# Chunked attention and a feed-forward on one core: the opening stretch in another order, with more zero products

## The chip, the cores and the metric

The kernel runs on one core of one Trainium2 chip. The metric is the device time of one execution in microseconds. Before the change it is 223.09 us, the median of three runs (223.05 to 223.10).

## The reference

Four sequences (B) of 768 tokens with 8 heads of 64. Each chunk of 32 queries sees 8 memory keys and the keys from 16 before to 8 after the chunk; the result, put together over the heads, goes through a normalization and two weight matrices, and is added to itself.

```python
for c in range(nc):                       # chunks of 32
    l_start, r_end = max(0, c_start - 16), min(S, c_end + 8)
    k_full = concat(mem_k, k[l_start:r_end]); v_full = concat(mem_v, v[l_start:r_end])
    a = softmax(q_c @ k_full.T / 8)
    out[c] = a @ v_full
x = out, heads side by side               # (4, 768, 512)
xn = (x - mean) / sqrt(var + 1e-6) * g_ln
y = x + relu(xn @ w_ch1) @ w_ch2          # 512 -> 2048 -> 512
```

## The kernel before, in words

**Tiles and units.** The tokens are 24 tiles of 128 (6 for each sequence). The feed-forward goes by units u = 0 to 7 of three tiles. W1 (`w1c`) and W2 (`w2c`) lie in SBUF as four quarters each. For a unit, "up" makes the 2048 hidden columns (xT times a quarter of W1, then a relu into `rT`), "down" multiplies them by W2 and adds up over the quarters. Attention of later tiles is put between these steps.

**Attention of a tile.** `scores` are 16 products of 64 x 104 x 64 into a PSUM pair `att`; `soften` are two exponentials on ScalarE (into `AT`); `values` are 16 products with V, followed on VectorE by a reciprocal, a scaling that also sums, and the negative mean; `norm` subtracts the mean and multiplies by `gb` (the gain, spread over 128 partitions by two products `spread_g`); `turn_x` transposes the result into `xT`, for the first tiles by four products on TensorE and a copy on VectorE. The division by the standard deviation comes at the very end, since relu lets it through.

**Keys and queries.** They arrive in blocks of 256 tokens. A block of raw data (`st`) is rearranged by one copy (`mix`, or `mix_raw` in pieces for the first block, into `iv`), transposed by eight products (`transpose_block`, `first_q`), and copied out of PSUM: keys by `window` and `key_left`, `key_right` into `KT` with its overlapping windows; queries by `part_q` or `whole_q` into `QR`. The memory keys go through `mem_keys` (16 small transposes), `memT` and `mem_cols` into KT's last columns; the memory values through `v_mem` into V.

**The order.** There is no scheduler: each engine carries out its instructions in the order in which the program calls the helpers, and semaphores carry the data dependencies. The program has a front written out by hand (lines 557 to 627) and a plan of 28 steps for each unit (`at`, `attend`). Unit 0 is special: `up_tile(u, c, i, eng)` makes all 512 hidden columns of quarter c for one tile i alone, in 16 products of 128 columns, so that work can begin when the first tile is done. The front calls it for tiles 0 and 1 of all four quarters, and the loop for tile 2 in steps 12 to 15. From step 16 come the down products. PSUM for up and down products are four banks `mm`, taken in turn by `slot`.

**Zero products.** `warm(n, m, p)` multiplies zeros by zeros into a bank that nobody reads. They are there to keep TensorE active while it has nothing else to do.

**Loads.** `first_load`, the memory keys, the gain and the memory values go by the queues of SyncE, ScalarE and GpSimd at the very start; everything else goes by GpSimd's queue in one fixed order: second key block, V, W1's first quarter, V, W1's second, second query block, W1's third, V, W1's last, third key block, V, W2's first quarter, and so on. Each issue there waits for the landing of the eighth load before it.

Of the kernel before, what the change touches and what calls it, by code (L numbers as in the profile page):

```python
# [15 lines left out]
def kernel(  # L16
# [12 lines left out]
    nc = tc.nc  # L29
# [60 lines left out]
    def dram(t, offset, pattern):  # L90
        return bass.AP(tensor=t.tensor, offset=offset, ap=[list(p) for p in pattern])

    def free(ap, off, pattern, parts=None):
        p = list(ap.ap[0]) if parts is None else [ap.ap[0][0], parts]
        return bass.AP(tensor=ap.tensor, offset=ap.offset + off, ap=[p] + [list(x) for x in pattern])
# [4 lines left out]
    def copy(eng, out, in_):  # L100
        if eng is nc.scalar:
            eng.copy(out=out, in_=in_)
        else:
            eng.tensor_copy(out=out, in_=in_)
# [28 lines left out]
    def v_mem(b, g0, g1, eng):  # L133
        src = memv16[96:W, b, :, :]
        copy(eng, free(V[b % 2][96:W, g0:g1, :, :], 0, [[H * VW, g1 - g0], [1, H * VW]]),
             bass.AP(tensor=src.tensor, offset=src.offset,
                     ap=[list(src.ap[0]), [0, g1 - g0], [1, H * VW]]))
# [12 lines left out]
    def mem_keys():  # L150
        p = slot("att")
        pv = as16(p[:, 0, :])
        for m in range(8):
            for par in range(2):
                nc.tensor.matmul(
                    out=pv[64 * par : 64 * par + 64, 32 * m : 32 * m + 32],
                    lhsT=memk16[:, 64 * m : 64 * m + 64], rhs=identity[0:32, 0:32],
                    is_transpose=True, start=True, stop=True, tile_position=(0, 64 * par),
                )
        mem_slot.append(pv)  # L160
# [52 lines left out]
    def transpose_block(b, blk, which, banks):  # L213
        i = pick(iv, ("b", b, blk, which))
        for r in range(8):
            pv = banks[r // 4 if len(banks) == 2 else 0]
            c = 128 * (r % 4 if len(banks) == 2 else r)
            nc.tensor.matmul(  # L218
                out=pv[:, c : c + 128], lhsT=i[:, 128 * r : 128 * r + 128], rhs=identity,
                is_transpose=True, start=True, stop=True,  # L220
            )
# [26 lines left out]
    def part_q(b, blk, half, pv, eng):  # L248
        copy(eng, free(QR[b % 2], 1024 * blk + 64 * half, [[128, 8], [1, 64]]),
             free(pv, 64 * half, [[128, 8], [1, 64]]))  # L250

    def mix_raw(which, srcs, half, eng, lo=0, hi=128):

        o = pick(iv, ("b", 0, 0, which))[lo:hi, :]
        r0, n = (0, 8) if half is None else (4 * half, 4)
        for par in range(2):
            copy(eng, free(o, 128 * r0 + 64 * par, [[128, n], [1, 64]]),
                 free(srcs[par][lo:hi, :], 64 * r0, [[64, n], [1, 64]]))

    def first_q(half):  # L260

        i = pick(iv, ("b", 0, 0, 1))
        rows = slice(64 * half, 64 * half + 64)
        for r in range(8):
            c = 128 * r + 64 * half
            nc.tensor.matmul(
                out=Q0[0][:, c : c + 64],
                lhsT=i[rows, 128 * r : 128 * r + 128], rhs=identity[rows, rows],
                is_transpose=True, start=True, stop=True, tile_position=(64 * half, 0),
            )  # L270
# [33 lines left out]
    def soften(b, t, c):  # L304
        p = score_slot[b, t]
        nc.scalar.activation(  # L306
            out=free(AT[t % 3], 32 * c, [[64, 16], [1, 32]]),
            in_=free(p, 4 * c, [[64, 16], [1, 4], [8, 8]], W),
            func=ACTF.Exp, bias=band[0:W, c : c + 1], scale=0.125,
        )  # L310
# [45 lines left out]
    def turn_x(b, t):  # L356
        i = NT * b + t
        dst = xT[(i // 3) % 2][:, :, 128 * (i % 3) : 128 * (i % 3) + 128]
        if i not in ON_PE:
            nc.sync.dma_start_transpose(out=dst, in_=xn[i % 4])  # L360
            return
        p = slot("att")
        pv = as16(p[:, 0, :])
        for dt in range(4):
            nc.tensor.matmul(  # L365
                out=pv[:, 128 * dt : 128 * dt + 128],
                lhsT=xn[i % 4][:, 128 * dt : 128 * dt + 128], rhs=identity,
                is_transpose=True, start=True, stop=True,
            )
        nc.vector.tensor_copy(out=dst, in_=free(pv, 0, [[128, 4], [1, 128]]))  # L370
# [10 lines left out]
    def relu(eng, o, p):  # L381
        if eng is nc.scalar:
            nc.scalar.activation(out=o, in_=p, func=ACTF.Relu)  # L383
        else:
            nc.vector.tensor_scalar(out=o, in0=p, scalar1=0.0, scalar2=None, op0=ALU.max)  # L385
# [12 lines left out]
    def up_tile(u, c, i, eng):  # L398
        p = slot("mm")
        for k_ in range(4):  # L400
            for dt in range(4):
                nc.tensor.matmul(  # L402
                    out=p[:, 128 * k_ : 128 * k_ + 128],
                    lhsT=free(w1c[c][:, dt, :], k_, [[4, 128]]),
                    rhs=xT[u % 2][:, dt, 128 * i : 128 * i + 128],
                    start=(k_ == 0 and dt == 0), stop=(k_ == 3 and dt == 3),
                )
        relu(eng, rT[c][:, :, 128 * i : 128 * i + 128], free(p, 0, [[128, 4], [1, 128]]))

    down_slot = {}  # L410

# [40 lines left out]
    def warm(n, m=512, p=None):  # L452
        p = mm[3] if p is None else p
        for _ in range(n):
            nc.tensor.matmul(out=p[:, 0:m], lhsT=zero[:, 0:128], rhs=zero[:, 0:m], start=True, stop=True)
# [4 lines left out]
    def first_load(which, par, lo, hi, eng):  # L460
        eng.dma_start(
            out=raws[which][par][4 * lo : 4 * hi, :],
            in_=dram((k, q)[which], 4 * par * HS + 512 * lo, [[512, hi - lo], [HS, 4], [1, 512]]),
        )

    first_load(0, 0, 0, 32, nc.sync)
    first_load(0, 1, 0, 32, nc.scalar)
    first_load(1, 0, 0, 16, nc.sync)
    first_load(1, 1, 0, 16, nc.gpsimd)
    nc.sync.dma_start(out=memkf, in_=dram(mem_k, 0, [[512, 32], [1, 512]]))  # L470
    nc.sync.dma_start(out=grow, in_=dram(moe_g_ln, 0, [[512, 1], [1, 512]]))

    nc.sync.dma_start(out=xs[5][96:W, :], in_=dram(mem_v, 0, [[64, 8], [512, 8], [1, 64]]))
# [80 lines left out]
        cols = slice(256 * half, 256 * half + 256)  # L554
        nc.tensor.matmul(out=mm[3][:, cols], lhsT=gone, rhs=grow[:, cols], start=True, stop=True)

    warm(7)
    mix_raw(0, raws[0], 0, dve)
    mix_raw(0, raws[0], 1, act)
    transpose_block(0, 0, 0, K0)  # L560
    mix_raw(1, raws[1], 0, dve, 0, 64)
    mix_raw(1, raws[1], 1, act, 0, 64)
    copy(dve, memk16, memkf)
    first_q(0)
    mem_keys()
    window(0, 0, K0, 0, dve)
    window(0, 0, K0, 1, act)
    part_q(0, 0, 0, Q0[0], act)
# [9 lines left out]
    mix(0, 1, 0, dve)  # L578
    spread_g(1)
    first_q(1)  # L580
    part_q(0, 0, 1, Q0[0], dve)
    copy(act, gb, mm[3])
    values(0, 0)
    norm(0, 0)
    window(0, 0, K0, 2, act)
# [2 lines left out]
    window(0, 1, Q0, 0, act)  # L588
    window(0, 1, Q0, 1, act)
    key_right(0, 3, act)  # L590
    turn_x(0, 0)
    warm(1, 512, mm[1])
    scores(0, 1)
    soften(0, 1, 0)
    soften(0, 1, 1)
    v_mem(0, 2, 4, dve)
    turn["mm"] = 3
    up_tile(0, 0, 0, act)
    values(0, 1)
    norm(0, 1)  # L600
    window(0, 1, Q0, 2, dve)
    window(0, 1, Q0, 3, act)
    key_left(0, 4, dve)
    warm(1, 512, mm[1])
    mix(0, 1, 1, dve)
    up_tile(0, 1, 0, act)
    turn_x(0, 1)
    Q1 = [as16(slot("mm")) for _ in range(2)]
    transpose_block(0, 1, 1, Q1)
    whole_q(0, 1, Q1)  # L610
    up_tile(0, 0, 1, act)
    scores(0, 2)
    soften(0, 2, 0)
    soften(0, 2, 1)
    v_mem(0, 4, 6, dve)
    up_tile(0, 1, 1, dve)
    up_tile(0, 2, 0, dve)
    values(0, 2)
    norm(0, 2)
    up_tile(0, 2, 1, act)  # L620
    mix(0, 2, 0, dve)
    up_tile(0, 3, 0, act)
    turn_x(0, 2)
    up_tile(0, 3, 1, dve)
    total(cnt[:, 1:2], 0, 80)
    total(cnt[:, 2:3], 96, W)
    nc.vector.tensor_tensor(out=cnt[:, 1:2], in0=cnt[:, 1:2], in1=cnt[:, 2:3], op=ALU.add)
    plan = {}

    def at(u, step, fn, *args):  # L630
# [97 lines left out]
    for u in range(8):  # L728
        for step in range(U):
            if step < 16:  # L730
                if u == 0:
                    if step >= 12:
                        up_tile(0, step - 12, 2, dve if step % 2 else act)
                else:
                    up(u, step)
            elif u == 0:
                c, i = divmod(step - 16, 3)
                down(u, i, c)
            else:
                i, c = divmod(step - 16, 4)  # L740
                if u == 7 and i == 2:
                    if c == 0:
                        last_down(u, i)
                else:
                    down(u, i, c)
            for fn, args in sorted(plan.get((u, step), ()), key=lambda x: x[0] is not soften or x[1][2] == 0):
                fn(*args)
# [30 lines left out]
```

## Time and profile before

| | |
|---|---|
| time | 223.09 us |
| span of the profile | 221.3 us |
| TensorE busy | 212.3 us (96%), 1969 products |
| VectorE, ScalarE, GpSimd busy | 133.2, 102.1, 97.5 us |
| largest groups on TensorE | L417 down 83.0 us, L391 up (units 1 to 7) 78.5, L402 up tiles of unit 0 13.4 |
| chain that ended last | TensorE 80% of the span |

TensorE is the engine to look at. Its row in the 40 slices is 9 (90% or more) almost everywhere except in the first four slices. Column "PEclk" of that table shows what a throttle granted, not the rate at which the products really ran: that has to be read from the distance of like products. In the timelines, a line gives the start, the length, the engine, the line of the program, what is written and read, the shape and the number of instructions, and in brackets the idle time of the engine just before and what ended it. In the windows, each engine has its busy time and the number of its instructions, and the last three columns are the granted clock, the share of the DMA engines that was busy, and GB/s.

### The profile page before, as it was taken

What the parts mean: (1) busy time and instruction counts of PE and PEld (TensorE: products, weight loads), DVE (VectorE), ACT (ScalarE), POOL (GpSimd) and SP (SyncE); (2) the same over time, 40 slices, a digit from 0 to 9 for tenths busy, and PEclk for the clock granted to TensorE, in tenths of its full rate; (3) what the DMA queues carried; (4) which work ended last, traced back from release to release, by engine and by line L of the source; (5) the groups of instructions that cost most, each with busy time, mean ns of one, the idle gap of its engine ahead of it and who ended that gap; (6) DMA issues with size and microseconds to landing.
All of it is one profiled execution on the core that took longest, in us unless ns stands there. A gap on an engine that the chain in (4) does not pass through costs nothing.

```text
span 221.3 us, 4995 instructions
## 1 busy us (share of the span) xinstructions
PE 212.3 (96%) x1969; PEld 131.4 (59%) x1969; DVE 133.2 (60%) x329; ACT 102.1 (46%) x217; POOL 97.5 (44%) x171
## 2 busy tenths in 40 slices
PE   5978999999999999999999999999999999999993
PEld 1656986557755576546754576446754666456553
DVE  5755686587879768735756687716754377234221
ACT  3554558516783167623771176424841466103200
POOL 7954496798897991303832893200011011100000
PEclk9999999999999999999999999999999999999999
DMA  6999999999979999277995899693112211210012
GB/s 169 173 190 195 197 195 192 183 140 222 157 100 151 222 184 156 45 175 168 145 153 102 102 156 187 64 204 99 27 24 79 90 23 27 71 69 29 0 47 95
DMA packets 72274, 27.70 MB, mean 125 GB/s; under 512 B 60346, under 2 KB 68282, under 8 KB 72251
## 3 DMA queue, kind: packets, MB, share of 16 engines
q0 software_dynamic: 46080, 14.71, 62.9%
q1 hardware_dynamic: 26026, 12.41, 25.5%
q8 instruction: 15, 0.25, 0.5%
q10 hardware_dynamic: 144, 0.26, 0.4%
q14 instruction: 9, 0.07, 0.1%
HBM read 30.28 MB, written 6.29 MB: 165 GB/s over the span
## 4 chain that ended last, share of the span: by engine, by line
PE 80%; DVE 0%; issue 0%; DVEq 0%
PE mm L417 34%; PE mm L391 34%; PE att L296 5%; PE att L317 3%; PE mm L439 2%; PE att L218 1%; PE mm L218 1%; PE att L365 0%; DVE osb L444 0%; DVEq L444 0%
## 5 line engine op out<-in xcount | busy, mean ns | idle before, releaser
L417 PE MATMUL mm<-w2c,rT 128*128 128x512 f16 x368 | 83.0, 379 | 0.0
L391 PE MATMUL mm<-xT,w1c 128*128 128x384 f16 x448 | 78.5, 327 | 0.0
L391 PEld LDWEIGHTS <-w1c 128*128 128x128 f16 x448 | 49.0, 114 | 22.0
L417 PEld LDWEIGHTS <-rT 128*128 128x128 f16 x368 | 34.9, 98 | 39.4
L385 DVE TENSOR_SCALAR rT<-mm 128x384 f16<-128x384 f32 (+1 forms) x61 | 34.3, 567 | 25.7 <-PE mm L391 22.3
L383 ACT ACTIVATE rT<-mm 128x384 f16<-128x384 f32 (+1 forms) x63 | 31.4, 503 | 38.6 <-PE mm L391 22.6
L306 ACT ACTIVATE AT<-att,band 104x512 f16<-104x512 f32 x48 | 31.3, 684 | 29.8 <-PE att L296 29.8
L128 POOL DMA_DIRECT2D V<-in_v_dram x48 | 38.8, 822 | 7.2 <-DMA w1c<-in_moe_w_ch_dram 4.3
L426 DVE SCALAR_TENSOR_TENSOR osb<-mm,rstd,xs 128x512 f32<-128x512 f32 x23 | 17.2, 749 | 33.5 <-PE mm L417 27.5
L348 POOL TENSOR_SCALAR veps<-sq 128x1 f32<-128x1 f32 x24 | 7.4, 310 | 63.4 <-ACT junk L342 49.8
L342 ACT ACTIVATE junk<-xs,nmean 128x512 f16<-128x512 f32 x24 | 17.3, 722 | 15.4 <-DVE nmean L331 13.4
L337 DVE SCALAR_TENSOR_TENSOR xn<-xs,nmean,gb 128x512 f16<-128x512 f32 x24 | 17.9, 747 | 0.5
L325 DVE SCALAR_TENSOR_TENSOR xs<-att,rec 128x512 f32<-128x512 f32 x24 | 16.6, 691 | 0.8
L296 PE MATMUL att<-QR,KT 64*104 64x64 f16 x384 | 16.0, 235 | 0.1
L296 PEld LDWEIGHTS <-KT 64*104 64x104 f16 x384 | 12.7, 135 | 4.7 <-issue 3.4
L352 POOL TENSOR_TENSOR rstd<-veps,mhalf 128x1 f32<-128x1 f32 x24 | 14.5, 603 | 2.0
L120 POOL DMA_DIRECT2D st<-in_q_dram x22 | 13.1, 618 | 4.1 <-DMA st<-in_q_dram 2.3
L120 POOL DMA_DIRECT2D st<-in_k_dram x22 | 12.8, 605 | 2.8 <-DMA w1c<-in_moe_w_ch_dram 2.7
L402 PE MATMUL mm<-xT,w1c 128*128 128x128 f16 x192 | 13.4, 232 | 0.0
L324 DVE RECIPROCAL rec<-att 128x8 f32<-128x8 f32 x24 | 4.9, 206 | 13.2 <-PE att L317 12.8
L317 PEld LDWEIGHTS <-AT 104*64 104x64 f16 x384 | 8.4, 114 | 7.3 <-issue 3.9
L402 PEld LDWEIGHTS <-w1c 128*128 128x128 f16 x192 | 12.3, 118 | 0.5 <-issue 0.3
(77 smaller groups left out, 144.0 us busy)
## 6 DMA issues: line engine op xcount, KB each, us to landing
out_dram<-osb SPq DMA_DIRECT2D x23, 256.0 KB, 2.2
V<-in_v_dram POOLq DMA_DIRECT2D x40, 96.0 KB, 5.7
st<-in_k_dram POOLq DMA_DIRECT2D x22, 128.0 KB, 5.9
st<-in_q_dram POOLq DMA_DIRECT2D x22, 128.0 KB, 6.6
w1c<-in_moe_w_ch_dram POOLq DMA_DIRECT2D x4, 512.0 KB, 11.1
w2c<-in_moe_w_ch_dram POOLq DMA_DIRECT2D x4, 512.0 KB, 8.5
V<-in_v_dram POOLq DMA_DIRECT2D x8, 80.0 KB, 5.4
xT<-xn SPq DMA_TRANSPOSE x17, 2.4
```

Source lines behind the costliest of these rows:

```text
L120: nc.gpsimd.dma_start(out=s[:, 512 * par : 512 * par + 512], in_=dram((k, q)[which], (b * H + 4 * par) * HS + blk * 256 * D, [[512, 32], [ ...
L128: nc.gpsimd.dma_start(out=V[b % 2][lo:hi, g, :, 0:64], in_=dram(v, b * H * HS + (64 * g - 16 + lo) * D, [[64, hi - lo], [HS, H], [1, 64]]),)
L296: nc.tensor.matmul(out=p[0:W, par, (4 * gg + j) * 64 : (4 * gg + j) * 64 + 64], lhsT=KT[b % 2][rows, 2 * t + gg, j, :], rhs=free(QR[b % 2] ...
L306: nc.scalar.activation(out=free(AT[t % 3], 32 * c, [[64, 16], [1, 32]]), in_=free(p, 4 * c, [[64, 16], [1, 4], [8, 8]], W), func=ACTF.Exp, ...
L337: nc.vector.scalar_tensor_tensor(out=xn[i % 4], in0=xs[i % 9], scalar=nmean[t], in1=gb, op0=ALU.add, op1=ALU.mult,)
L342: nc.scalar.activation(out=junk, in_=xs[(NT * b + t) % 9], func=ACTF.Square, bias=nmean[t], scale=1.0, accum_out=sq[t],)
L383: nc.scalar.activation(out=o, in_=p, func=ACTF.Relu)
L385: nc.vector.tensor_scalar(out=o, in0=p, scalar1=0.0, scalar2=None, op0=ALU.max)
L391: nc.tensor.matmul(out=p, lhsT=free(w1c[c][:, dt, :], i, [[4, 128]]), rhs=xT[u % 2][:, dt, 128 * lo : 128 * (lo + n)], start=(dt == 0), st ...
L402: nc.tensor.matmul(out=p[:, 128 * k_ : 128 * k_ + 128], lhsT=free(w1c[c][:, dt, :], k_, [[4, 128]]), rhs=xT[u % 2][:, dt, 128 * i : 128 * ...
L417: nc.tensor.matmul(out=p, lhsT=rT[c][:, k_, 128 * i : 128 * i + 128], rhs=w2c[c][:, k_, :], start=(c == 0 and k_ == 0), stop=(c == 3 and k ...
L426: nc.vector.scalar_tensor_tensor(out=o, in0=p, scalar=rstd[t % 9], in1=xs[t % 9], op0=ALU.mult, op1=ALU.add,)
```

## The change

It reorders the front and moves some operations to other engines; what is computed and the loads stay, apart from one place in SyncE's queue. The parts:

1. Ten zero products instead of seven before the first transposes, and one more ahead of the memory keys' transposes.
2. The memory keys are loaded second on SyncE's queue, cast before the first queries, and transposed before them.
3. The copy of the gain `gb` from PSUM goes from ScalarE to VectorE, before the copy of the second half of the first queries.
4. `scores(0, 1)` and its exponentials come before `turn_x(0, 0)`, with three zero products ahead of them instead of one behind the turn; the last key windows of block 1 come before the first up tile, and the zero product after `values(0, 1)` goes.
5. `mix` of the second query block goes from VectorE to ScalarE.
6. The relu of `up_tile(0, 1, 0)` goes from ScalarE, where it stood right after its products, to VectorE after `scores(0, 2)`; for this `up_tile` can give back its operands instead of issuing the relu.
7. `up_tile(0, 0, 1)` goes from before `scores(0, 2)` to after it.
8. The two up tiles of W1's last quarter for tiles 0 and 1 leave the front. The loop takes six up tiles from step 10 on: tile 2 for the first three quarters, then all three tiles for the last.

Parts 1 and 2 are meant to have TensorE at its full rate early and the first scores sooner; 3 to 7 to fit the order to that; 8 so as not to wait for the load of W1's last quarter.

```diff
-        relu(eng, rT[c][:, :, 128 * i : 128 * i + 128], free(p, 0, [[128, 4], [1, 128]]))
+        pair = rT[c][:, :, 128 * i : 128 * i + 128], free(p, 0, [[128, 4], [1, 128]])
+        if eng is None:
+            return pair
+        relu(eng, *pair)
...
+    nc.sync.dma_start(out=memkf, in_=dram(mem_k, 0, [[512, 32], [1, 512]]))
     first_load(1, 0, 0, 16, nc.sync)
     first_load(1, 1, 0, 16, nc.gpsimd)
-    nc.sync.dma_start(out=memkf, in_=dram(mem_k, 0, [[512, 32], [1, 512]]))
...
-    warm(7)
+    warm(10)
     mix_raw(0, raws[0], 0, dve)
     mix_raw(0, raws[0], 1, act)
     transpose_block(0, 0, 0, K0)
+    copy(dve, memk16, memkf)
+    warm(1)
+    mem_keys()
     mix_raw(1, raws[1], 0, dve, 0, 64)
     mix_raw(1, raws[1], 1, act, 0, 64)
-    copy(dve, memk16, memkf)
     first_q(0)
-    mem_keys()
...
     first_q(1)
+    copy(dve, gb, mm[3])
     part_q(0, 0, 1, Q0[0], dve)
-    copy(act, gb, mm[3])
     values(0, 0)
...
     key_right(0, 3, act)
-    turn_x(0, 0)
-    warm(1, 512, mm[1])
+    warm(3, 512, mm[1])
     scores(0, 1)
     soften(0, 1, 0)
     soften(0, 1, 1)
+    turn_x(0, 0)
     v_mem(0, 2, 4, dve)
-    turn["mm"] = 3
-    up_tile(0, 0, 0, act)
-    values(0, 1)
-    norm(0, 1)
     window(0, 1, Q0, 2, dve)
     window(0, 1, Q0, 3, act)
     key_left(0, 4, dve)
-    warm(1, 512, mm[1])
-    mix(0, 1, 1, dve)
-    up_tile(0, 1, 0, act)
+    turn["mm"] = 3
+    up_tile(0, 0, 0, act)
+    mix(0, 1, 1, act)
+    values(0, 1)
+    norm(0, 1)
+    late = up_tile(0, 1, 0, None)
     turn_x(0, 1)
     Q1 = [as16(slot("mm")) for _ in range(2)]
     transpose_block(0, 1, 1, Q1)
     whole_q(0, 1, Q1)
-    up_tile(0, 0, 1, act)
     scores(0, 2)
     soften(0, 2, 0)
     soften(0, 2, 1)
+    relu(dve, *late)
     v_mem(0, 4, 6, dve)
+    up_tile(0, 0, 1, act)
     up_tile(0, 1, 1, dve)
-    up_tile(0, 2, 0, dve)
     values(0, 2)
     norm(0, 2)
+    up_tile(0, 2, 0, act)
     up_tile(0, 2, 1, act)
+    turn_x(0, 2)
     mix(0, 2, 0, dve)
-    up_tile(0, 3, 0, act)
-    turn_x(0, 2)
-    up_tile(0, 3, 1, dve)
...
+    TILES = ((0, 2), (1, 2), (2, 2), (3, 0), (3, 1), (3, 2))
...
                 if u == 0:
-                    if step >= 12:
-                        up_tile(0, step - 12, 2, dve if step % 2 else act)
+                    if step >= 10:
+                        up_tile(0, *TILES[step - 10], dve if step % 2 else act)
```

## The prediction

> **What bounds the kernel now.** I read the busy table in 40 slices first (TensorE 9 in every slice from the fifth on), then the waits of TensorE, then windows cut where its work changes, then its timeline, then the DMA issues.
>
> The waits of TensorE (time, times, longest) and the windows (busy time of each engine in each stretch):
>
> ```profile
> PE mm L218 <- DVE iv L104: 2.0, 2, 1.2
> PE att L365 <- DVE xn L337: 1.7, 3, 1.2
> ```
> ```profile
> 22.19:29.04 6.85, 6.52 (x125) 6.07 (x126) 4.58 (x11) 3.83 (x7) 4.07 (x7) 1.00 1.42 198
> 29.04:34.65 5.61, 5.61 (x107) 5.45 (x105) 4.32 (x15) 3.56 (x12) 5.40 (x13) 1.00 1.58 190
> 34.65:49.20 14.55, 14.32 (x152) 7.80 (x151) 9.96 (x27) 7.58 (x16) 11.12 (x20) 1.00 1.33 171
> ```
>
> From 22 us on TensorE hardly stops; after 44 us no wait of it is listed at all. So the end moves by what the front (up to the first down product at 34.65) gains or loses, and by nothing else. The front's own timeline on TensorE (start, length, line, operation):
>
> ```profile
> 15.65 0.91 PE L296 MATMUL att<-QR,KT 64*104 64x64 f16 x16
> 16.49 1.90 PE L402 MATMUL mm<-xT,w1c 128*128 128x128 f16 x16
> ...
> 22.19 0.62 PE L218 MATMUL mm<-identity,iv 128*128 128x128 f16 x8 [0.79 <-DVE iv L104]
> 22.65 1.06 PE L402 MATMUL mm<-xT,w1c 128*128 128x128 f16 x16
> 23.64 0.65 PE L296 MATMUL att<-QR,KT 64*104 64x64 f16 x16
> 24.22 1.98 PE L402 MATMUL mm<-xT,w1c 128*128 128x128 f16 x32
> 26.12 0.44 PE L317 MATMUL att<-V,AT 104*64 104x65 f16 x16
> 26.50 1.98 PE L402 MATMUL mm<-xT,w1c 128*128 128x128 f16 x32
> 28.80 0.40 PE L365 MATMUL att<-identity,xn 128*128 128x128 f16 x4 [0.33 <-DVE xn L337]
> 29.04 1.95 PE L402 MATMUL mm<-xT,w1c 128*128 128x128 f16 x32
> ```
>
> Two things are to be seen. The same 16 products of an up tile take 1.90 at 16.49 and 1.06 at 22.65: TensorE runs at half speed until some point near 20 us (the granted-clock column says 1.00 throughout and doesn't show it). And between 22.65 and 34.65 every chain of other engines is covered by up tiles, of 0.89 us each (1.95 for two, less the drain).
>
> The loads are on GpSimd's queue. Issued at 8.89 and 9.43, the second query block (st) lands 10.5 us later; W1's last quarter is issued at 14.87:
>
> ```profile
> st<-in_q_dram POOLq DMA_DIRECT2D x2, 128.0 KB, 10.5
> ```
> ```profile
> w1c<-in_moe_w_ch_dram POOLq DMA_DIRECT2D x1, 512.0 KB, 11.5
> ```
>
> So the query block is complete at 19.95 and W1's last quarter at 26.4. The order of loads is not changed, and each issue waits for an earlier load, not for TensorE, so I keep both.
>
> [...] (1.90-0.31)/15 = 106 ns a product before, (1.06-0.22)/15 = 56 ns after. [...] the trace has TensorE busy from 10.0 to 13.5 with transposes and narrow products, and still at half speed afterwards[...]. [...] VectorE's rearrangement of the query block starts at 21.45, 1.5 us after the block landed, behind a norm and two copies. [...] ScalarE's relus here take 0.60 for 512 columns and 0.49 for 384, or 0.86.
>
> **The change part by part.**
>
> *Zero products, mem keys first.* Ten products at 427 ns from 1.18 end at 5.45; the first transposes start at 5.55, when VectorE has the keys, so three more cost nothing. One more stands in the wait for the mem keys' cast. The aim is the clock: [...] Both branches are carried. With mem keys cast ahead of the queries, VectorE reaches the first scores about 0.35 sooner (9.0 instead of 9.39).
>
> *gb on VectorE.* A 128x512 f32 read from PSUM is 0.69 there (row of L385), between the cast of the second queries and values(0,0), where ScalarE had 0.58. It eats what the earlier scores gave VectorE: values' reciprocal at 12.35 cold or 11.85 hot, against 12.63. ScalarE's key copies, freed of gb, still wait for the second block's transposes and end at about 14.5 cold, 13.5 hot.
>
> *Scores ahead of turn_x, three zero products.* scores(0,1) then starts at 14.55 cold or 13.6 hot, against 15.65. But cold, turn_x after it makes up(0,0) start at 16.5, as before; hot, 15.0. W1's second quarter (issued at 8.14, 10.7 later, so 18.9) then stops a hot TensorE in any case, for up(1,0).
>
> *Query rearrangement on ScalarE.* It no longer stands behind the norm: it starts when the block lands, 19.98. ScalarE has not run a 1024-column copy here; bounds are VectorE's 0.69 and two 512-column copies, 1.2. I take 0.60 + 512 x 0.86 ns = 1.04: done at 21.04, transposes at 21.1 hot. Cold, turn_x(0,1) (about 21.03, as before) is in front and they start at 21.26. Before: 22.19. So this step gains 0.9 to 1.1, and the clock decides only 0.16 of it. The landing is what caps it.
>
> *What follows the transposes.* Here is the loss. Before, up(0,1) lay between the transposes and scores(0,2), and two tiles of W1's last quarter, (3,0) and (3,1), lay before tile 2's first product. Now the first is behind the scores and the others are behind three tiles of tile 2. With intervals of the old timeline, hot:
> - Transposes to query copy done on ScalarE: 22.19 to 23.43, so 21.1 to 22.33; scores(0,2) at 22.38. TensorE has 0.45 of work in it and then waits 0.83.
> - Scores to both exponentials done: 0.69 + 1.26, at 24.33. TensorE goes on after 0.58, does up(0,1) and up(1,1) in 1.90, and starts values(0,2) at 24.86. ScalarE relus up(0,1) behind the exponentials, nobody waits for it.
> - VectorE has relu(1,1), 0.75 from 24.97, queued ahead of the reciprocal: that starts at 25.66; reciprocal to norm takes 1.90 (26.84 to 28.74): 27.56. The deferred relu of up(1,0) runs at 22.0 and meets up(1,1)'s need of its buffer at 23.9 without a wait.
> - TensorE: 0.38 for values, two tiles 1.79, at 27.03; turn_x at 27.62. A wait of 0.59, in which W1's last quarter has been there since 26.4 and isn't asked for.
> - turn_x 0.23, then VectorE's copy: 0.50 to its start, 0.42, 0.06: tile 2 may start at 28.60. A wait of 0.75.
> - From there, six tiles instead of five: 29.04 to 34.65 was 5.61 with five tiles, the eight transposes and the scores; with one more, 6.50. First down product at 35.10.
>
> Against 34.65 this is +0.45 hot and +0.6 cold. The 1.1 gained at 21.1 is paid back with 1.7 of waits that were covered before. After 34.65 the order on all engines is the same, TensorE is busy 14.32 of 14.55, and the second matrix' first quarter (landing at 31.4) is not reached sooner, so the shift is carried to the end. I take +0.5: 223.09 + 0.5 = 223.6.
>
> **The rivals.**
> - *A wash.* If values(0,2) isn't held by up(1,1) and the reciprocal not by the relu, the chain runs on its own links: values at 24.4, norm done at 26.75, tile 2 free at about 28.0 after the two tiles; six tiles then end at 34.5. With the cold variant's 0.16 this is between -0.15 and 0: 223.0. For it: each hold is under half a microsecond and rests on a place in a queue. Against: the order on both engines is fixed and the durations are of this trace.
> - *Faster.* The gain of the transposes stands and TensorE isn't starved, because the query block lands sooner than 19.95 or the chain is much shorter: 223.09 - 1.1 = 222.0. For it: the waits of 0.79 and 1.16 us go[...]. Against: what runs at half speed there hangs on casts, copies and landings; every load in flight shares queues that are busy in every slice.
> - *The clock goes wrong.* A hot TensorE with little to do from 16.4 to 21.1 falls back[...] Against: before had waits of 0.4 and 0.8 within 2 us and stayed at full speed.
>
> **How the numbers follow.** Starved as worked out 0.50, a wash 0.22, faster 0.13, clock 0.15. The predicted time is the first case's, 223.6. Its unknowns are the ScalarE copy (0.69 to 1.2: -0.35 to +0.15), the branch of the clock (0.16) and the landing (some 0.3 either way). Slower by over 0.45 us (0.2%): most of the first case (0.40 of 0.50) and all of the clock, 0.55; within: the rest of the first and most of the wash, 0.27; faster: 0.13 and the wash's edge, 0.18. The range runs from the better half of the faster side of the wash to the clock's edge, 222.4 to 224.4, leaving out most of the faster case and half of the clock's.
>
> **What would show it.** Right: the second block's query transposes at 21.0 to 21.3, ended by ScalarE's copy that started within 0.1 of the landing near 19.95; three new waits of TensorE between 21.5 and 28.6, of about 0.8 (ScalarE's or VectorE's query copy), 0.6 (norm) and 0.75 (copy of xT); first down product near 35.1; the stretch from it to the end as long as before. Wrong: a down product before 34.5, or transposes of the queries before 20.8 (the landing is not the cap), or up tiles of 1.9 us after 20.3 (the clock). Whether an up tile at 15 to 16.5 takes 1.06 or 1.90 tells if the zero products did what they are for; by these sums it matters for 0.16 us.

## The result and the profile after

The changed kernel takes 224.29 us (median of 4 runs, 223.93 to 224.94) against 223.07 us (223.04 to 223.10): ratio 1.0058, 95% interval 1.0035 to 1.0081. Run again beside the next experiments it is 224.28 against 223.19, ratio 1.0040 (1.0024 to 1.0055). It is slower, by 1.1 to 1.2 us.

Waits of TensorE in the trace of after (us in total, times, longest):

```profile
PE mm L402 <- DVE xT L370: 1.5, 2, 1.0
PE mm L458 <- DVE zero L511: 1.2, 1, 1.2
PE att L296 <- ACT QR L102: 1.1, 2, 0.7
PE att L365 <- DVE xn L337: 1.1, 1, 1.1
```

The timeline of TensorE in the trace of after, from the second scores to tile 2:

```profile
15.89 1.05 PE L402 MATMUL mm<-xT,w1c 128*128 128x128 f16 x16 [0.51 <-DVE xT L370]
16.88 0.44 PE L317 MATMUL att<-V,AT 104*64 104x65 f16 x16
17.25 1.09 PE L402 MATMUL mm<-xT,w1c 128*128 128x128 f16 x16
19.43 0.40 PE L365 MATMUL att<-identity,xn 128*128 128x128 f16 x4 [1.09 <-DVE xn L337]
19.66 0.61 PE L218 MATMUL mm<-identity,iv 128*128 128x128 f16 x8
20.95 0.65 PE L296 MATMUL att<-QR,KT 64*104 64x64 f16 x16 [0.67 <-ACT QR L102]
21.53 3.28 PE L402 MATMUL mm<-xT,w1c 128*128 128x128 f16 x32
24.74 0.65 PE L317 MATMUL att<-V,AT 104*64 104x65 f16 x16
25.32 1.98 PE L402 MATMUL mm<-xT,w1c 128*128 128x128 f16 x32
27.43 0.40 PE L365 MATMUL att<-identity,xn 128*128 128x128 f16 x4
28.83 2.87 PE L402 MATMUL mm<-xT,w1c 128*128 128x128 f16 x48 [1.00 <-DVE xT L370]
```

Up tiles run at full rate from 15.9 on (1.05), so the opening is faster: the second query block's transposes start at 19.66 instead of 22.19. Behind them TensorE waits 0.67 and 1.00 us, and the two tiles at 21.53 take 3.28 us instead of 1.98: half rate again. Windows of that trace, cut at the clock's edges (us, TensorE busy and products, granted clock, DMA share, GB/s):

```profile
11.70:15.12 3.41, 3.41 (x36) 0.50 1.68 193
15.12:18.53 3.41, 2.70 (x52) 1.00 1.22 200
18.53:21.94 3.41, 1.84 (x35) 1.00 1.68 186
21.94:25.36 3.41, 3.41 (x45) 0.50 1.46 193
```

Since the first loads land up to 0.7 us apart from one trace to the next, the traces are best compared by distances. F is the start of the first transposes, S that of the second query block's transposes, D that of the first down product (from the timelines, in us; D to the end is the span less D; each ratio is to before as run beside it):

| trace | F to S | S to D | D to end | time, ratio to before (95%) |
|---|---|---|---|---|
| before | 16.64 | 12.46 | 186.65 | |
| before, second trace | 16.27 | 12.45 | 186.65 | |
| after | 13.74 | 15.71 | 186.8 | 224.29, 1.0058 (1.0035 to 1.0081) |
| after, second trace | 15.31 | 14.38 | 186.7 | 224.28, 1.0040 (1.0024 to 1.0055) |
| last quarter back | 14.99 | 13.14 | 186.9 | 222.88, 0.9989 (0.9975 to 1.0004) |
| kept busy | 15.84 | 14.38 | 186.7 | 224.50, 1.0055 (1.0036 to 1.0075) |
| seven zeros | 14.13 | 15.87 | 186.7 | 224.43, 1.0055 (1.0038 to 1.0073) |
| old tail | 15.71 | 12.67 | 186.6 | 222.48, 0.9968 (0.9955 to 0.9980) |
| old tail, gb on ScalarE | 13.84 | 12.68 | 186.8 | 221.51, 0.9930 (0.9903 to 0.9957) |
| the same, filled | 14.25 | 12.87 | 186.9 | 221.69, 0.9924 (0.9910 to 0.9938) |
| before, ten zeros | 16.16 | 12.45 | 186.9 | 222.69, 0.9982 (0.9971 to 0.9992) |
| before, query block on ScalarE | 16.39 | 12.45 | 186.7 | 223.03, 0.9993 (0.9980 to 1.0006) |
| before, windows and query block | 15.52 | 12.74 | 186.6 | 222.64, 0.9966 (0.9953 to 0.9978) |

D to the end hardly moves: everything is decided before the first down product, and the change gains in the first column and loses more in the second. A gain in the first column is not all the change's own: the second traces of after and of before differ from the first ones too.

### The profile page after: what moved, and what is told of

It reads as the page before. It is cut to its first block, busy times and chain, and to the rows that moved or that the text cites. A ratio compares the mean times of both kernels' runs of the same rounds, so it can differ in the third digit from the quotient of the medians.

```text
span 222.2 us, 5004 instructions
## 1 busy us (share of the span) xinstructions
PE 212.9 (96%) x1974; PEld 131.7 (59%) x1974; DVE 133.8 (60%) x329; ACT 102.8 (46%) x217; POOL 98.5 (44%) x171
## 4 chain that ended last, share of the span: by engine, by line
PE 79%; DVE 0%; issue 0%; DVEq 0%
PE mm L420 34%; PE mm L391 34%; PE att L296 5%; PE att L317 3%; PE mm L442 2%; PE att L218 1%; PE mm L218 1%; PE att L365 0%; DVE osb L447 0%; DVEq L447 0%
## 5 line engine op out<-in xcount | busy, mean ns | idle before, releaser
L342 ACT ACTIVATE junk<-xs,nmean 128x512 f16<-128x512 f32 x24 | 17.4, 725 | 15.1 <-DVE nmean L331 10.8
L120 POOL DMA_DIRECT2D st<-in_k_dram x22 | 13.4, 636 | 2.1 <-DVE KT L104 2.0
L120 POOL DMA_DIRECT2D st<-in_q_dram x22 | 12.5, 589 | 2.2 <-DMA st<-in_q_dram 1.0
L102 ACT COPY KT<-rawk 128x352 f16<-128x352 f16 (+1 forms) x12 | 9.0, 812 | 5.7 <-DMA rawk<-iv 5.7
```

What stands on the lines that cost most here:

```text
L120: nc.gpsimd.dma_start(out=s[:, 512 * par : 512 * par + 512], in_=dram((k, q)[which], (b * H + 4 * par) * HS + blk * 256 * D, [[512, 32], [ ...
L342: nc.scalar.activation(out=junk, in_=xs[(NT * b + t) % 9], func=ACTF.Square, bias=nmean[t], scale=1.0, accum_out=sq[t],)
```

## The experiments

**1. The changed kernel again.** No edit.

> The changed kernel unaltered, for a second trace. [...] the clock edges (4.88, 8.29, 15.12, 21.94, 25.36 us in the first trace) stand elsewhere, still a multiple of 3.413 us apart, and the times scatter over some 223.9 to 224.9 us. If the edges are tied to the program, they stand at the same places and the time is within 0.1 us of 223.9.

Measured: 224.28 us, 12 runs from 223.06 to 224.61. The edges of the granted clock stand at 10.39 and 20.63 in this trace, at 8.29, 15.12, 21.94 and 25.36 in the first. TensorE's timeline:

```profile
18.81 1.90 PE L402 MATMUL mm<-xT,w1c 128*128 128x128 f16 x16
20.99 0.40 PE L365 MATMUL att<-identity,xn 128*128 128x128 f16 x4 [0.28 <-DVE xn L337]
21.23 0.61 PE L218 MATMUL mm<-identity,iv 128*128 128x128 f16 x8
22.51 0.65 PE L296 MATMUL att<-QR,KT 64*104 64x64 f16 x16 [0.67 <-ACT QR L102]
23.09 1.98 PE L402 MATMUL mm<-xT,w1c 128*128 128x128 f16 x32
24.99 0.44 PE L317 MATMUL att<-V,AT 104*64 104x65 f16 x16
25.37 1.98 PE L402 MATMUL mm<-xT,w1c 128*128 128x128 f16 x32
27.68 0.40 PE L365 MATMUL att<-identity,xn 128*128 128x128 f16 x4 [0.33 <-DVE xn L337]
29.07 2.87 PE L402 MATMUL mm<-xT,w1c 128*128 128x128 f16 x48 [1.00 <-DVE xT L370]
```

Here the clock doesn't fall in the tail (the tiles at 23.09 take 1.98), and the time of this profiled run (224.10) is no better than that of the first (223.93). So the change is slow without the fall too. The waits of 0.67 and 1.00 stand in both. In the first trace the granted clock stands at 0.50 from 8.29 to 15.12 and from 21.94 to 25.36, in this one from 10.39 to 20.63: 10.24 us in each, and the means of the two are 0.977 and 0.976 (half of 10.24 in a span of 222 is 0.023). In eleven of the twelve runs it is 0.975 to 0.977, as in both traces; the twelfth, at 0.984, took 223.06 us and so no longer than before.

**2. Before again.** No edit.

> The kernel before, for a second trace. Theory 'the change moved the loads': the second query block lands at 19.9 to 20.0 us again. Theory 'the landings differ from run to run or chip to chip': it lands at 18.2, as in the trace of after, and the time is still 223.1, because the block waits behind VectorE's norm until 21.4 in either case.

Measured: 223.29 us, a single run; the query block lands at 18.7 instead of 19.95. The landings differ between traces of one kernel (18.7 and 20.0 for before, 18.2 and 19.1 for after; 17.4 to 20.0 over all traces here), so the 18.2 in the trace of after is not the change's doing. One line of TensorE's waits (us in total, times, longest) tells what the block's arrival was worth:

```profile
PE mm L218 <- ACT KT L102: 0.6, 1, 0.6
```

The block was there 1.2 us earlier, and its transposes gained 0.37 (F to S 16.27 against 16.64), with the full rate 1.5 us earlier as well (18.75 against 20.25): their banks were freed by ScalarE's key copy.

**3. The last quarter back.**

```diff
     up_tile(0, 2, 1, act)
+    up_tile(0, 3, 0, act)
     turn_x(0, 2)
     mix(0, 2, 0, dve)
+    up_tile(0, 3, 1, dve)
...
-                    if step >= 10:
-                        up_tile(0, *TILES[step - 10], dve if step % 2 else act)
+                    if step >= 12:
+                        up_tile(0, step - 12, 2, dve if step % 2 else act)
```

> The changed kernel with one part undone: up tiles (3,0) and (3,1) are back in the front, around the turn of tile 2, ahead of tile 2's first product. Theory 'order' (TensorE is starved since covering tiles stand behind the wait): the waits between 27.1 and 28.8 us go, 1.3 us less, time 222.6 to 223.2, ratio to before about 0.999. Theory 'clock' (the loss is the fall to half speed near 22 us): that is settled before these tiles; at most 0.3 us less, time 223.9 to 224.5.

Measured: 222.88 us. Its timeline has three tiles in a row and no wait listed around the turn of tile 2:

```profile
25.25 2.87 PE L402 MATMUL mm<-xT,w1c 128*128 128x128 f16 x48
27.96 0.39 PE L365 MATMUL att<-identity,xn 128*128 128x128 f16 x4
28.18 2.26 PE L402 MATMUL mm<-xT,w1c 128*128 128x128 f16 x32
```

What is left of the wait lies inside the last line: two tiles take 2.26 instead of 1.95, so 0.3 us. The time is 1.4 us less, S to D 13.14 instead of 14.38, with the rates as in the second trace of after (full rate from 20.5): as theory "order" expected, and over four times what "clock" allowed.

**4. Kept busy.**

```diff
     late = up_tile(0, 1, 0, None)
+    warm(3, 512, mm[0])
     turn_x(0, 1)
...
     whole_q(0, 1, Q1)
+    warm(3, 512, mm[0])
     scores(0, 2)
```

> The changed kernel with three zero products more ahead of the turn of tile 1 and three ahead of scores(0,2), in the waits of 1.1 and 0.7 us there. They do no work. Theory 'clock': [...] the clock doesn't fall, the two tiles after scores(0,2) take 1.95 us instead of 3.28, 1.3 us less, time 222.6 to 223.2. Theory 'order': waits stay waits, time within 0.3 us of after.

Measured: 224.50 us, not told from after. In its trace the full rate came at 20.5, about where it came in experiment 1 (20.63), and there no fall followed without the extra products either (the tiles at 23.09 took 1.98); as a test of a prevented fall it says nothing. It does say that filling the waits without work brought nothing here.

**5. The old tail.** From the second query block's transposes on the order of before, with the opening of after. The deferred relu stays, and `mix` of the third key block stays behind `turn_x`:

```diff
     whole_q(0, 1, Q1)
+    up_tile(0, 0, 1, act)
     scores(0, 2)
...
-    up_tile(0, 0, 1, act)
     up_tile(0, 1, 1, dve)
+    up_tile(0, 2, 0, dve)
     values(0, 2)
     norm(0, 2)
-    up_tile(0, 2, 0, act)
     up_tile(0, 2, 1, act)
+    up_tile(0, 3, 0, act)
     turn_x(0, 2)
     mix(0, 2, 0, dve)
+    up_tile(0, 3, 1, dve)
```

with the loop as in experiment 3.

> The changed kernel with the order of before from the second query block's transposes on: up(0,1) ahead of scores(0,2), up(2,0) ahead of values(0,2), (3,0) and (3,1) around the turn of tile 2. The opening, the deferred relu and the query rearrangement on ScalarE stay. Theory 'order': the whole loss is in the tail; the opening's gain of about 1 us (transposes at 21.1 to 21.3 instead of 22.2 to 22.4) is kept, first down product near 33.7, time 222.0 to 222.4. Theory 'opening' (zero products and new order of the opening cost as well): no gain over the variant with the last quarter alone back, 222.7 to 223.1.

Measured: 222.48 us, ratio 0.9968: faster than both. S to D is 12.67, 0.2 from before. The full rate came at 20.8, so the clock of the tail is that of the second trace of after, where S to D is 14.38. The loss is in the tail's order, and the opening is worth having. One of its waits led to experiment 9:

```profile
PE mm L218 <- DVE QR L104: 0.8, 1, 0.8
```

**6. Before, with the query block on ScalarE.**

```diff
     up_tile(0, 0, 0, act)
+    mix(0, 1, 1, act)
     values(0, 1)
...
     warm(1, 512, mm[1])
-    mix(0, 1, 1, dve)
     up_tile(0, 1, 0, act)
```

> The kernel before with one edit: the second query block is rearranged by ScalarE, right after the first up tile's relu. If the gain ahead of the transposes is this step's alone, they start at 21.1 to 21.4 instead of 22.2 to 22.4 and the time is 222.0 to 222.4, as for the variant with the old tail. If the other edits of the opening are needed for it, the time stays within 0.3 us of before.

Measured: 223.03 us, no difference. The transposes started at 22.31, and these lines of its timeline, ScalarE's and TensorE's, say why:

```profile
21.77 0.49 ACT L102 COPY KT<-mm 128x160 f16<-128x160 f16 x2 [1.53 <-DVE KT L104]
22.31 0.61 PE L218 MATMUL mm<-identity,iv 128*128 128x128 f16 x8 [0.61 <-ACT KT L102]
```

They write the banks from which ScalarE still had to copy the last key window, and that copy waits for VectorE's, which stood behind the norm. Moving the rearrangement alone removes one of two waits that end within 0.2 us of each other in the trace of before (21.97 and 22.13).

**7. Seven zeros.** The changed kernel with `warm(7)` and without the zero product ahead of `mem_keys`.

> The changed kernel with seven zero products at the start and none ahead of the memory keys. If the zero products bring what they are for, it is slower than after by 0.2 us or more; by the prediction's sums they are worth 0.16 us when they take effect, so 223.9 to 224.6, not told from after. No full-rate stretch before 15 us.

Measured: 224.43 us, not told from after, as the prediction's sums had it. But the reason was another: its trace went to the full rate at 15.5 without the extra products (the up tile at 16.48 takes 1.05), and fell at 22.3 (the two at 22.12 take 3.47). The end of `values`, block 1's transposes, the three zero products of part 4 and scores(0,1) leave no gap from 12.09 to 15.51 (busy 3.42 of 3.42 us); that this brought the rate is not shown.

**8. Before, ten zeros.** `warm(10)` for `warm(7)`.

> The kernel before with ten zero products instead of seven and nothing else. Full rate for one window of 3.4 us from between 4.8 and 7 us on, then half rate until about 18 to 21 us; the time within 0.3 us of before, since casts, copies and landings set the order there.

Measured: 222.69 us, ratio 0.9982: 0.4 us better than before, a little more than expected. Full rate from 4.5 us to about 7.9, so 3.4 us of it (the first transposes take 0.62, where before has 1.03), and then half rate to 18.1 (the up tile at 16.19 takes 1.90, that at 18.66 1.06). Why that helps is not shown: F to S is 16.16 in its trace, S to D that of before.

**9. gb on ScalarE.** The old tail, and

```diff
-    copy(dve, gb, mm[3])
     part_q(0, 0, 1, Q0[0], dve)
+    copy(act, gb, mm[3])
```

> The variant with the old tail, and gb copied by ScalarE again, after the query copy. Theory 'gb on VectorE costs': the wait of 0.8 us ahead of block 1's transposes (ended by VectorE's query copy, which stands behind gb) shrinks to 0.1 to 0.3, time 0.3 to 0.6 us below the variant with the old tail, 221.9 to 222.2. Theory 'hidden': nothing waits on that chain, the time is within 0.15 us of 222.5.

Measured: 221.51 us, ratio 0.9930, the lowest median here. More than the 0.3 to 0.6 expected: block 1's transposes follow `values` without a gap, TensorE was busy from 11.0 to 15.4, and the full rate came at 14.8 in this trace (the up tile at 16.00 takes 1.05). In that of experiment 5, with the wait behind gb in this place, it came at 20.8 (the one at 17.03 takes 1.87); but the edges of the clock lie elsewhere there (10.53 and 20.77), so that the wait prevented it is not shown. The runs go by the clock: four of the six have a mean of 0.984, as in this trace, and took 220.97 to 221.77; the two at 0.977 and 0.968 took 222.78 and 222.88. Of experiment 5's 22 runs, six have 0.984 or more (221.19 to 222.45). So part of the gain goes with the higher granted clock, which more of these runs have; what the shorter wait is worth by itself is not told apart.

**10. Filled.** Experiment 9 with `warm(1, 512, mm[0])` ahead of `up_tile(0, 0, 0)` and of `turn_x(0, 1)`.

> The same with one more zero product ahead of the first up tile and one ahead of the turn of tile 1, so that TensorE has no gap over 0.2 us between block 1's transposes and the second quarter's tile. [...] the full rate is there from 17.5 us at the latest in every trace, most often from 14 to 15 us, and the time is 221.2 to 222.0 with less scatter than the variant without. If gaps are not what keeps the clock down, no change, within 0.2 us of that variant.

Measured: 221.69 us, ratio 0.9924; not told from experiment 9 in the middle, with less spread (221.36 to 222.14). The full rate was there at 15.85 (the up tile takes 1.05), and all six runs have a mean granted clock of 0.982 to 0.990. What it waits for has become the loads:

```profile
17.71 1.08 PE L402 MATMUL mm<-xT,w1c 128*128 128x128 f16 x16 [0.44 <-DMA w1c<-in_moe_w_ch_dram]
...
26.30 1.08 PE L402 MATMUL mm<-xT,w1c 128*128 128x128 f16 x16 [0.73 <-DMA w1c<-in_moe_w_ch_dram]
```

The second line is up(3,0), held by W1's last quarter: the wait that part 8 of the change was made against. It is in no other trace here, and costs 0.73 where part 8 costs 1.4.

**11. Before, windows and query block.** Experiment 6 with `window(0, 1, Q0, 2, dve)`, `window(0, 1, Q0, 3, act)` and `key_left(0, 4, dve)` moved ahead of `up_tile(0, 0, 0)`.

> The kernel before with two edits: the last key windows of block 1 come ahead of the first up tile, and the second query block is rearranged by ScalarE. In the trace with the second edit alone the transposes waited 0.6 us for ScalarE's key copy, which frees their bank. Theory 'both waits': from the first transposes of the front to those of the second query block 15.7 us or less instead of 16.3 to 16.6, time 222.2 to 222.7 (about 0.6 us less than before). Theory 'the clock or the mem keys brought it': no change, within 0.2 us of before.

Measured: 222.64 us, ratio 0.9966, F to S 15.52. So the two moves together give as much as the old tail with the whole new opening. The move of the key windows alone was not tried, and it may hold much of this: on VectorE they stand just ahead of the rearrangement, from 20.87 to 21.45 in the trace of before, so without them it would start 0.58 us sooner, an estimate from these two times, and ScalarE's key copy, which ends at 18.90 in the trace here, would be out of the way as well.

## Why the prediction was right, and where it was off

- **Direction and mechanism: right, with some luck.** Slower, because tiles that covered waits stand behind them. The sequence of the sum is in the second trace of after nearly to the figure. Its cold branch (TensorE still at half rate) had the transposes at 21.26; measured 21.23. Adding the sum's intervals to that start, scores(0,2) come at 22.54 (22.51), values(0,2) at 25.02 (24.99) and turn_x at 27.78 (27.68). Experiments 3 and 5 show it by taking it back: 1.4 us for the tiles of the last quarter, 1.7 in all with the rest of the old tail (1.09 above before to 0.58 below; S to D 14.38 to 12.67). The luck: that trace starts 0.37 later than the one that the sum was made from (F 5.92 against 5.55), so that 21.23 met 21.26 with an opening 0.40 shorter. And the first trace came to the same time another way, by a faster opening and the fall of the clock; its transposes at 19.66 are what the prediction had named as a sign that the landing is not the cap.
- **The three waits: two of them.** About 0.8 behind the query copy was 0.67, 0.75 behind the copy of xT was 1.00. The third, 0.6 for the norm, is no new one: 0.33 in the second trace of after, none in the first, and 0.33 at 28.80 in before as well, where the prediction called every chain covered. From values(0,2) to turn_x it is 2.69 in the second trace (24.99 to 27.68) and 2.68 in before (26.12 to 28.80).
- **Size: too small, and the term that was mis-sized is the copy of xT.** From turn_x to tile 2 the sum had 0.50 + 0.42 + 0.06, 0.98; measured 1.39 in the second trace (27.68 to 29.07) and 1.40 in the first. VectorE's line in the trace of after:

```profile
28.35 0.42 DVE L370 COPY xT<-att 128x512 f16<-128x512 f16 x1 [0.97 <-ACT rT L383]
```

  It starts 0.92 after the transposes instead of 0.50. The ScalarE relu named there had ended at 27.94, so it isn't what the copy waited for. The same copy was late in every trace with this order and in that of experiment 3, and prompt in those of before and of experiment 5; why was not settled. With it, S to D is 14.38 where the sum gave 14.00 (21.10 to 35.10). That is 0.4 of the 0.6 to 0.7 by which the forecast of +0.5 fell short. The sum is not closed by it, since the opening of the same trace is 0.40 shorter than forecast: from F to D it is 29.69 against the sum's 29.71 (35.26 less 5.55), while the two traces of before have 29.10 and 28.72. The rest stays open; it is of the size by which traces of one kernel differ.
- **The clock as a rival: half right.** The fall near 22 us did come, in the first trace and in that of experiment 7, where S to D is 15.7 and 15.9. It was to add 0.9 to the sum, for 224.5, which was the author's estimate. S to D is 1.3 to 1.5 longer with it, but the traces in which it comes are those in which the full rate at 15 us had made the opening 1.2 to 1.6 us shorter, and these two runs took 223.93 and 224.55, beside 224.10 without it. The prediction had allowed for a hot TensorE (one at full rate) that falls back; but by its sum a hot opening was worth 0.16, so it had nothing to set against the fall.
- **"The landing is what caps it", so the clock decides 0.16: wrong in general.** 19.95 was one trace's landing; others have 17.4 to 19.5. With these the chain through up(0,0) and the norm sets the transposes, and the rate matters: F to S 13.7 to 14.3 in the four traces with the full rate by 16 us, 15.3 to 15.9 in three of the four others with all of the new opening (15.0 in experiment 3).
- **Query block on ScalarE, "0.9 to 1.1": right as a sum (F to S is 0.96 to 1.33 shorter in the second trace of after), wrong as a cause.** The copy took 1.04 as worked out, but experiment 6 shows that it gains nothing without the move of the key windows, to which the prediction had given no worth.
- **gb on VectorE: seen and undervalued.** It was noted to eat VectorE's lead; that block 1's transposes wait for what stands behind it was not followed up (0.8 to 0.9 us in three of the traces with it, 0.36 in one, none in the first of after and in experiment 7).
- **Faster, as a rival:** the opening's gain without the starvation was put at 222.0 and needed another tail. With that tail, experiments 5, 9 and 10 have 222.48, 221.51 and 221.69.
- **Slips in the sums.** "1.7 of waits" takes the gain of the hot branch and the loss of the cold one; within a branch it is 1.54 (14.00 less 12.46). The relu's 0.75 after 24.97 gives 25.72; 25.66 is with its 0.69. The waits of before said to be "0.4 and 0.8" are 0.19 and 0.79 in its timeline.

## What to carry to other kernels

When a chain of several engines stands between two pieces of TensorE work, count the pieces that are left to cover it: what is gained by bringing the chain's head forward is lost again if its cover goes behind its end. A wait that is put down to one releaser may have a second one ending just beside it; try each move alone, and both, before crediting either. Guarding against a late load by reordering costs its waits in every run, while the late load costs only when the rest is fast enough to meet it (0.73 against 1.4 us here).

## What the runs showed of the hardware

- The edges of the granted clock are multiples of 3.413 us apart in the trace of after (8.29, 15.12, 21.94, 25.36) and in its second trace (10.39, 20.63), and between the two they stand elsewhere; in the two traces of before the full rate came near 20.25 and 18.75 (up tiles of 1.90 at 16.49 and 1.82 at 17.14 ahead of it, of 1.06 at 22.65 and 19.49 behind it). The runs of experiment 9 with a mean granted clock of 0.984 and those with less lie 1.0 us or more apart.
- The full rate was lost without TensorE being idle for all of the 3.41 us before: in the trace of after the granted clock fell to 0.50 after 3.41 us with 1.84 busy (18.53 to 21.94), in experiment 7 after 1.65 busy (18.92 to 22.33), while it stayed at 1.00 after 2.25 (18.19 to 21.60) in experiment 9. Recorded busy time alone doesn't sort the cases: in the second trace of after it fell at 10.39 although TensorE had been busy 3.25 of 3.41, with narrow products and `spread_g`. What decides is not shown.
- Nor does busy time sort what stood ahead of a rise. The stretch 11.70 to 15.12 of after (3.41 busy: the end of `values`, eleven transposes, zero products and scores) was followed by the full rate, and so was one of 2.92 us of zero products and eight transposes (3.71 to 7.12 in experiment 5), while one of 2.90 us of zero products, scores, a turn and part of an up tile (13.95 to 17.36, same trace) was not. In the trace of before a stretch filled with transposes, values, `first_q` and `spread_g` (10.01 to 13.43, 3.41 busy) was not. Which of these products matter for it was not tried.
- In before the granted clock reads 1.00 in every stretch from 3.19 to 20.25, though the up tile at 16.49 took 1.90 and the one at 22.65 1.06. The distance of like products tells the rate: 106 and 56 ns.
